# Image scale weights loaded and used in two column parts, with V rows between

## The chip, the cores and the metric

The kernel runs on one core of a Trainium2 chip. The time is device time in microseconds (us) of one execution, the median of several. A core has four compute engines that run their own instruction streams and meet at semaphores: TensorE (PE in the profile; its weight loads are PEld), VectorE (DVE), ScalarE (ACT) and GpSimd (POOL). SyncE (SP) issues most of the transfers (DMAs) between main memory and the on-chip buffer SBUF. TensorE writes into PSUM, in eight banks; VectorE and ScalarE copy from there.

## The reference

One attention block for an image stream and a text stream, batch B = 2, 256 image tokens and 32 text tokens per batch, D = 1152 channels, all bf16:

```python
mod_i = (silu(c) @ wmod_img)          # six D-wide parts; shift, scale, gate are used
hi = layernorm(x_img) * (1 + sci) + shi
qi, ki, vi = split(hi @ wqkv_img)     # the same for the text stream
p = softmax(concat(qt, qi) @ concat(kt, ki).T * D**-0.5)
a = p @ concat(vt, vi)
out_i = x_img + gai * (ai @ wo_img)   # the same for the text stream
```

The weights are read once each: fourteen blocks of 1152 x 1152, some 37 MB, through five SBUF slots of one block.

## The kernel before

D is cut into KT = 9 blocks of P = 128 channels. The image tokens of both batches are 512 columns, in four token tiles (`i` = 0 to 3; 0 and 1 are the first batch). A weight block is a tile of 128 partitions by 9 rows (`kt`) by 1152 columns; "row" below is one `kt`.

Transfers. All weight loads stand in one list on SP's queue (lines 97 to 115): the image tokens `x_i` in two pieces, the image scale weights `w_sc_i` in five row pieces (99 to 101), the V weights `w_v_i` in four (102, 103), then whole blocks: image shift `w_sh_i`, `w_q_i`, `w_k_i`, text shift, text scale, text q, k and v, the two gates, the two output blocks. A load into a slot waits until the slot's former user is done; a load also waits for the landing of an earlier load whose semaphore it takes over (eight loads before).

Order of the work. `pin` keeps an instruction at its place in its engine's program; matmuls (`mm`) and transposes (`tr`) are all pinned, so TensorE runs in the order of the source.

1. Warm-up matmuls on zeros (line 130, eight; line 145, fifteen) while `x_i` loads. `silu(c)` is computed and transposed into `sT`.
2. Layer norm of the image tokens (248 to 258). Tiles 0 and 2 get their sums on ScalarE (`ln_sums`, two activations), tiles 1 and 3 their statistics on VectorE (`ln_stats`, three `bn_stats` and an aggregate). `ln_norm` on VectorE writes the normalized tiles `xn_i`.
3. Transposes of `xn_i` by TensorE into PSUM, three channel blocks of one batch at a time (`x_transposes`), copied out into `xT_i`. Before, the three groups of the first batch go ahead of the scale matmuls and those of the second batch between them (259 to 272).
4. Image scale, `sc_cols`: 81 matmuls with two output columns each, 9 rows by 9 column blocks, accumulated in one PSUM bank `sc_ps`; `warm_up(3)` and `warm_up(1)` stand between the row pieces. Then VectorE adds 1 (273).
5. `x_scale` on VectorE multiplies the transposed tokens by 1 + scale into `hS_i`, one channel block of one batch at a time (274 to 280).
6. V: `v_open` multiplies `hS_i` with `w_v_i` into PSUM banks of 512 columns (281 to 284): A0 is token tiles 0 and 1 by two column chunks, A1 tiles 2 and 3 by the first chunk, six banks in all. The two left, (2,1) and (3,1), follow. `evac` copies a finished bank into `v_i`, alternately by VectorE and ScalarE.
7. Image shift (305, 306): `mod_rows_of(w_sh_i)` is 36 matmuls into `p_sh` (the group `gps` of the profile), transposed by VectorE into columns. They modulate `xT_i` in place on VectorE and ScalarE (310 to 317), and their product with `w_v_i` (`shift_v_rows`) makes up for the shift left out of V. The (2,1) bank runs around this stage (307, 319), (3,1) behind it.
8. q and k of the image, with the text stream's steps hooked in between, each with its own weight block: text shift, text scale, text q and k, v; then scores and softmax, the gate rows (`mod_rows`, again `gps`), attention and the output projections.

PSUM has two pools: `ps_mm` with six banks and `ps_tr` with two.

Of the kernel before, what the change touches and what calls it, by code (L numbers as in the profile page):

```python
# [8 lines left out]
ACT = mybir.ActivationFunctionType  # L9
ALU = mybir.AluOpType  # L10
# [4 lines left out]
def kernel(  # L15
# [14 lines left out]
    nc = tc.nc  # L30
    bf = mybir.dt.bfloat16
    f32 = mybir.dt.float32
    PSUM = bass.MemoryType.PSUM

    B, NI, D = x_img.shape
    NT = x_txt.shape[1]
    P = 128
    KT = D // P
# [4 lines left out]
    CH = 384  # L43
    NCH = D // CH
# [7 lines left out]
    const = ctx.enter_context(tc.tile_pool(name="const", bufs=1))  # L52
    work = ctx.enter_context(tc.tile_pool(name="work", bufs=2))
    small = ctx.enter_context(tc.tile_pool(name="small", bufs=4))
    ps_mm = ctx.enter_context(tc.tile_pool(name="ps_mm", bufs=6, space=PSUM))
    ps_tr = ctx.enter_context(tc.tile_pool(name="ps_tr", bufs=2, space=PSUM))

    pin = tc.keep_in_program_order

    def mm(*a, **k):  # L60
        return pin(nc.tensor.matmul(*a, **k))  # L61

    def tr(*a, **k):
        return pin(nc.tensor.transpose(*a, **k))  # L64
# [6 lines left out]
    x_i = act.tile([P, NIT, D], bf)  # L71
# [4 lines left out]
    def wtile(slot):  # L76
        return wpool.tile([P, KT, D], bf, tag="w%d" % slot, name="t")

    def wview(src, c0):
        return src.rearrange("(kt p) n -> p kt n", p=P)[:, :, c0:c0 + D]  # L80

    K8 = KT - 1

    def load_w(slot, src, c0, splits=(D,)):
        t = wtile(slot)
        sv = wview(src, c0)
        o = 0
        for n in splits:
            nc.sync.dma_start(t[:, :, o:o + n], sv[:, :, o:o + n])
            o += n  # L90
        return t

    w_sc_i = wtile(0)
    w_v_i = wtile(1)
    sc_v, v_v = wview(wmod_img, D), wview(wqkv_img, 2 * D)
    for b in range(B):
        nc.sync.dma_start(x_i[:, b * TPB:(b + 1) * TPB, :], x_img[b].rearrange("(p t) d -> p t d", t=TPB))  # L97

    SCC = (0, 3, 5, 7, K8, KT)
    for r0, r1 in zip(SCC, SCC[1:]):  # L100
        nc.sync.dma_start(w_sc_i[:, r0:r1, :], sc_v[:, r0:r1, :])  # L101
    for r0, r1 in ((0, 1), (1, 3), (3, 6), (6, KT)):
        nc.sync.dma_start(w_v_i[:, r0:r1, :], v_v[:, r0:r1, :])
    w_sh_i = load_w(2, wmod_img, 0)
    w_q_i = load_w(3, wqkv_img, 0)
    w_k_i = load_w(4, wqkv_img, D)
    w_sh_t = load_w(0, wmod_txt, 0)
    w_sc_t = load_w(1, wmod_txt, D)
# [17 lines left out]
    def warm_up(n):  # L126
        for _ in range(n):
            mm(wps[:], lhsT=warm[:, 0:P], rhs=warm[:], start=True, stop=True)
# [13 lines left out]
    sT_ps = ps_tr.tile([P, B * KT], bf, tag="tr")  # L142
    tr(sT_ps[:], s18[:], ident[0:B * KT, 0:B * KT])
    sT = const.tile([P, KT, B], bf)
    warm_up(15)

    def silu_cols():
        pin(nc.vector.tensor_copy(sT[:], sT_ps[:].rearrange("p (b kt) -> p kt b", b=B)))
# [4 lines left out]
    def evac(out_ap, in_ap):  # L153
        if evac_idx[0] % 2 == 0:
            nc.vector.tensor_copy(out_ap, in_ap)  # L155
        else:
            nc.scalar.copy(out_ap, in_ap)  # L157
        evac_idx[0] += 1

    def ln_stats(x_ap, np_, between=None):  # L160
        stats = small.tile([P, NCH, 6], f32, tag="stats")
        for k in range(NCH):
            if k == 1 and between:
                between()
            pin(nc.vector.bn_stats(stats[0:np_, k, :], x_ap[:, k * CH:(k + 1) * CH]))
        mv = small.tile([P, 2], f32, tag="mv")
        pin(nc.vector.bn_aggr(mv[0:np_, :], stats[0:np_, :, :]))
        return mv

    def ln_sums(x_ap, junk):  # L170
        sm = small.tile([P, 3], f32, tag="lnact")
        pin(nc.scalar.activation(junk, x_ap, ACT.Copy, scale=1.0 / D, accum_out=sm[:, 0:1]))
        pin(nc.scalar.activation(junk, x_ap, ACT.Square, scale=float(D) ** -0.5, accum_out=sm[:, 1:2]))
        return sm

    def ln_var(sm):
        pin(nc.vector.scalar_tensor_tensor(sm[:, 2:3], sm[:, 0:1], sm[:, 0:1], sm[:, 1:2],
                                           op0=ALU.mult, op1=ALU.subtract))
# [10 lines left out]
    xn_i = act.tile([P, NIT, D], bf, tag="A")  # L189
    hS_i = act.tile([P, KT, B * NI], bf, tag="Bt")  # L190
    xT_i = act.tile([P, KT, B * NI], bf)

    sc1_i = const.tile([P, KT, B], f32)
    qkT = act.tile([P, 2 * KT, B, NTOK], bf, tag="Q")

    sc_ps = ps_mm.tile([P, KT, B], f32, tag="mm")

    def sc_cols(r0, r1):
        for kt in range(r0, r1):
            for j in range(KT):  # L200
                mm(sc_ps[:, j, :], lhsT=w_sc_i[:, kt, j * P:(j + 1) * P], rhs=sT[:, kt, :],
                   start=(kt == 0 and j == 0), stop=(kt == KT - 1), skip_group_check=True)

    def x_transposes(k0, b):
        tr_pool = b == 0 and k0 < 6
        tp = (ps_tr if tr_pool else ps_mm).tile([P, 3, NI], bf, tag="tr" if tr_pool else "mm", name="tp")
        for kt in range(k0, k0 + 3):
            for t in range(TPB):
                i = b * TPB + t
                tr(tp[:, kt - k0, t * P:(t + 1) * P], xn_i[:, i, kt * P:(kt + 1) * P], ident[:])  # L210
        dst = xT_i[:, k0:k0 + 3, b * NI:(b + 1) * NI]

        def copy_out():
            pin(nc.scalar.copy(dst, tp[:]) if b == 0 or k0 == 6 else nc.vector.tensor_copy(dst, tp[:]))

        return copy_out

    def x_scale(k0, k1, b):
        for kt in range(k0, k1):
            pin(nc.vector.tensor_scalar(hS_i[:, kt, b * NI:(b + 1) * NI], xT_i[:, kt, b * NI:(b + 1) * NI],  # L220
                                        sc1_i[:, kt, b:b + 1], None, op0=ALU.mult))

    VW = 512
    v_i = act.tile([P, NIT, D], bf, tag="A")
# [2 lines left out]
    def v_open(ids, k0, k1, kt_major=True):  # L227
        for key in ids:
            if key not in accs:
                accs[key] = ps_mm.tile([P, VW], f32, tag="mm", name="vps")  # L230
        loop = [(kt, key) for kt in range(k0, k1) for key in ids] if kt_major else \
            [(kt, key) for key in ids for kt in range(k0, k1)]
        for kt, (i, cc) in loop:
            mm(accs[(i, cc)][:], lhsT=hS_i[:, kt, i * P:(i + 1) * P], rhs=w_v_i[:, kt, cc * VW:(cc + 1) * VW],
               start=(kt == 0), stop=(kt == KT - 1), skip_group_check=True)
            if kt == KT - 1:
                evac(v_i[:, i, cc * VW:(cc + 1) * VW], accs[(i, cc)][:])

    A0 = [(0, 0), (1, 0), (0, 1), (1, 1)]
    A1 = [(2, 0), (3, 0)]  # L240
# [4 lines left out]
    def ln_norm_act(i, sm):  # L245
        ln_norm(x_i[:, i, :], sm[:, 0:1], ln_rstd(sm[:, 2:3], P, sign=-1.0), P, xn_i[:, i, :])
# [3 lines left out]
    ln_var(s0)  # L250
    ln_norm_dve(1, m1)
    ln_norm_act(0, s0)
    s2 = ln_sums(x_i[:, 2, :], xn_i[:, 2, :])
    m3 = ln_stats(x_i[:, 3, :], P)
    ln_var(s2)
    r3, r2 = ln_rstd(m3[:, 1:2], P), ln_rstd(s2[:, 2:3], P, sign=-1.0)
    ln_norm(x_i[:, 3, :], m3[:, 0:1], r3, P, xn_i[:, 3, :])
    ln_norm(x_i[:, 2, :], s2[:, 0:1], r2, P, xn_i[:, 2, :])
    x_transposes(0, 0)()
    x_transposes(3, 0)()  # L260
    x_transposes(6, 0)()
    sc_cols(0, 3)
    warm_up(3)
    sc_cols(3, 5)
    warm_up(1)
    sc_cols(5, 7)
    x_transposes(0, 1)()
    out31 = x_transposes(3, 1)
    sc_cols(7, K8)
    sc_cols(K8, KT)  # L270
    out61 = x_transposes(6, 1)
    out61()
    pin(nc.vector.tensor_scalar_add(sc1_i[:], sc_ps[:], 1.0))
    x_scale(0, 3, 0)
    x_scale(0, 3, 1)
    out31()
    for b in range(B):
        x_scale(3, 6, b)
    for b in range(B):
        x_scale(6, KT, b)  # L280
    v_open(A0, 0, 3)
    v_open(A1, 0, 3)
    v_open(A0 + A1, 3, KT - 2)
    v_open(A0 + A1, KT - 2, KT, kt_major=False)

    NGG = 4
# [2 lines left out]
    def group(w, kt, g):  # L289
        return w[:, kt, :].rearrange("p (c g l) -> p g c l", g=NGG, l=LW)[:, g]  # L290

    def mod_rows_of(w, lhs):
        gps = ps_tr.tile([P, KT, LW], f32, tag="tr")
        for kt in range(KT):
            for g in range(NGG):
                mm(gps[LW * g:LW * g + LW], lhsT=lhs[:, kt, :], rhs=group(w, kt, g),
                   start=(kt == 0), stop=(kt == KT - 1), tile_position=(0, LW * g))
        return gps

    def mod_cols_of(gps, name):  # L300
        t = const.tile([P, KT, LW], f32, name=name)
        nc.vector.transpose(t[:].rearrange("p c l -> p (c l)"), gps[:].rearrange("p c l -> p (c l)"))
        return t

    p_sh = mod_rows_of(w_sh_i, sT32)
    sh_i = mod_cols_of(p_sh, "shc")
    v_open([(2, 1)], 0, 4)
    nc.vector.tensor_copy(shT32[:, :, 0:B], sh_i[:, :, 0:B])
    hT_i = xT_i
    for kt in range(KT):  # L310
        for b in range(B):
            h = hT_i[:, kt, b * NI:(b + 1) * NI]
            if b == 0 or kt % 3 == 0:
                nc.vector.tensor_scalar(h, h, sc1_i[:, kt, b:b + 1], sh_i[:, kt, b:b + 1],
                                        op0=ALU.mult, op1=ALU.add)
            else:
                nc.scalar.activation(h, h, ACT.Identity, bias=sh_i[:, kt, b:b + 1], scale=sc1_i[:, kt, b:b + 1])
    pin(nc.scalar.dma_start(x_t[:], xt_flat[:, :]))
    v_open([(2, 1)], 4, KT)
    v_open([(3, 1)], 0, KT)  # L320

    def v_last():
# [301 lines left out]
```

## Time and profile before

| | |
|---|---|
| median of five executions | 123.01 us (121.92 to 124.74) |
| the profiled execution | 121.92 us, span 120.1 us, mean granted TensorE clock 0.997 |
| TensorE busy | 113.7 us, 95% of the span |
| VectorE, ScalarE, GpSimd busy | 56.0, 34.5, 11.1 us |
| moved by DMA | 40.88 MB, mean 341 GB/s, about 410 GB/s until 98 us |
| first V matmul | 14.39 us |
| shift matmuls `gps` | 26.77 us |
| first q matmul | 35.20 us |

The span is the time from the first to the last instruction of the program; the execution takes 1.8 us more. A line of digits in the profile cuts the span in 40 slices and gives the busy share in tenths. Line 61 is the helper `mm`, so matmuls are told apart by the tiles they write. Ends of matmuls are modelled, starts are not; a row of n matmuls in the timeline runs to the end of its last one. In a row of a timeline, the engine, line, operation, output and inputs follow the start and the length, then the count. A row of DMA issues gives kilobytes and the time from issue to landing.

### The profile page before, as it was taken

Reading aid. Unit: us, or ns where it says so; the run is one execution under the profiler, and the core shown is the slowest. Engines: PE = TensorE matmul, PEld = TensorE weight load, DVE = VectorE, ACT = ScalarE, POOL = GpSimd, SP = SyncE. Lnnn points to the kernel's source line nnn. Section 1 sums busy time; section 2 is a strip of 40 time slices with the busy share of each in tenths; the row PEclk is TensorE's granted clock in tenths of the full one; section 3 lists DMA queues with packets and bytes.
Section 4 is the critical chain, followed back from the end, with each engine's and each line's share of the span. In section 5 each row is a group of like instructions: output and inputs, shape, how many; then the busy total and the mean of one; then the engine's idle time right before and its main releaser. Section 6 shows DMA issues by size and latency. Waiting matters only on the chain.

```text
span 120.1 us, 2599 instructions
## 1 busy us (share of the span) xinstructions
PE 113.7 (95%) x1112; PEld 67.4 (56%) x1121; DVE 56.0 (47%) x146; ACT 34.5 (29%) x73; POOL 11.1 (9%) x28
## 2 busy tenths in 40 slices
PE   5999899989999999999999999999999999999970
PEld 2248744435674444544548448486777766567650
DVE  1677590066837222131721203037885756666670
ACT  5799600054713103201011111125348610000000
POOL 7400000000000000000000000000222708000000
PEclk9999999999999999999999999999999999999998
DMA  3999999999999999999999999999999992420232
GB/s 129 372 389 389 406 405 408 416 408 415 403 369 412 404 409 414 411 411 412 407 411 411 418 401 414 411 405 411 411 400 411 411 359 68 138 98 0 98 81 72
DMA packets 18502, 40.88 MB, mean 341 GB/s; under 512 B 907, under 2 KB 1435, under 8 KB 18491
## 3 DMA queue, kind: packets, MB, share of 16 engines
q1 hardware_dynamic: 17616, 39.56, 84.6%
q0 software_dynamic: 480, 0.89, 2.2%
q10 hardware_dynamic: 395, 0.26, 0.7%
q8 instruction: 9, 0.15, 0.5%
q14 instruction: 2, 0.02, 0.0%
HBM read 39.38 MB, written 1.34 MB: 339 GB/s over the span
## 4 chain that ended last, share of the span: by engine, by line
PE 74%; DMA 20%; SPq 1%; DVE 1%; issue 1%
PE ps L61 51%; DMA t<-in_wmod_img_dram 20%; PE gps L61 6%; PE aps L61 6%; PE vps L61 5%; PE sps L61 4%; PE pT_ps L64 1%; SPq L97 1%; DVE tmp L565 1%; DVE o L566 0%; SPq L101 0%; PE tpt L64 0%
## 5 line engine op out<-in xcount | busy, mean ns | idle before, releaser
L61 PE MATMUL ps<-xT_i,t 128*128 128x512 bf16 x156 | 35.5, 379 | 0.4 <-issue 0.2
L61 PEld LDWEIGHTS <-t 128*128 128x128 bf16 x405 | 22.7, 98 | 19.3 <-issue 0.7
L61 PE MATMUL ps<-t,aT 128*128 128x384 bf16 (+3 forms) x153 | 20.2, 308 | 0.0
L61 PE MATMUL vps<-t,hS_i 128*128 128x512 bf16 (+1 forms) x106 | 17.8, 325 | 0.4 <-DVE hS_i L220 0.3
L61 PEld LDWEIGHTS <-aT 128*128 128x128 bf16 (+1 forms) x153 | 13.0, 101 | 7.1 <-issue 0.5
L61 PEld LDWEIGHTS <-hS_i 128*128 128x128 bf16 x108 | 9.0, 98 | 9.0 <-DVE hS_i L220 0.5
L155 DVE CAST qkT<-ps 128x512 bf16<-128x512 f32 (+1 forms) x6 | 3.8, 636 | 15.4 <-PE ps L61 15.4
L61 PE MATMUL wps<-warm 128*128 128x512 bf16 x26 | 8.9, 496 | 1.3 <-DVE warm L121 1.2
L435 POOL DMA_DIRECT2D mod_scratch<-g_sb x4 | 2.5, 633 | 80.1 <-ACT g_sb L157 80.1
L565 DVE TENSOR_TENSOR tmp<-ps,gb 128x384 bf16<-128x384 f32 (+2 forms) x13 | 6.8, 526 | 6.4 <-PE ps L61 6.3
L333 DVE TENSOR_SCALAR qkT<-ps 128x512 bf16<-128x512 f32 (+1 forms) x5 | 3.3, 665 | 10.8 <-PE ps L61 10.8
L335 ACT ACTIVATE qkT<-ps 128x512 bf16<-128x512 f32 (+1 forms) x6 | 3.3, 553 | 15.5 <-PE ps L61 15.5
L157 ACT CAST qkT<-ps 128x512 bf16<-128x512 f32 (+1 forms) x5 | 2.8, 565 | 16.6 <-PE ps L61 16.6
L155 DVE CAST v_i<-vps 128x512 bf16<-128x512 f32 x5 | 3.4, 689 | 7.9 <-PE vps L61 7.9
L61 PE MATMUL gps<-t,sT 128*32 128x288 bf16 x180 | 6.4, 287 | 0.5 <-DMA t<-in_wmod_img_dram 0.5
L61 PE MATMUL aps<-pT,v_i 128*128 128x288 bf16 x36 | 6.7, 287 | 0.0
L61 PEld LDWEIGHTS <-sT 128*32 128x32 bf16 x180 | 4.5, 96 | 2.5 <-issue 2.0
L61 PEld LDWEIGHTS <-warm 128*128 128x128 bf16 x27 | 2.9, 117 | 5.3 <-issue 2.9
L537 DVE TENSOR_SCALAR aT<-aps,svc 128x288 bf16<-128x288 f32 x9 | 4.7, 518 | 2.4 <-PE aps L61 2.3
L61 PE MATMUL sps<-qkT 128*128 128x288 bf16 (+1 forms) x54 | 5.5, 287 | 0.0
L157 ACT CAST v_i<-vps 128x512 bf16<-128x512 f32 x4 | 2.3, 586 | 10.6 <-PE vps L61 10.6
L539 ACT ACTIVATE aT<-aps,svc 128x288 bf16<-128x288 f32 x9 | 4.5, 502 | 2.5 <-PE aps L61 2.5
(94 smaller groups left out, 105.2 us busy)
## 6 DMA issues: line engine op xcount, KB each, us to landing
t<-in_wmod_txt_dram SPq DMA_DIRECT2D x3, 2592.0 KB, 18.9
t<-in_wqkv_txt_dram SPq DMA_DIRECT2D x3, 2592.0 KB, 15.5
t<-in_wmod_img_dram SPq DMA_DIRECT2D x2, 2592.0 KB, 18.9
t<-in_wqkv_img_dram SPq DMA_DIRECT2D x2, 2592.0 KB, 22.5
t<-in_wo_img_dram SPq DMA_DIRECT2D x1, 2592.0 KB, 18.2
t<-in_wo_txt_dram SPq DMA_DIRECT2D x1, 2592.0 KB
t<-in_wqkv_img_dram SPq DMA_DIRECT2D x2, 864.0 KB, 12.1
x_i<-in_x_img_dram SPq DMA_DIRECT2D x2, 576.0 KB, 4.1
```

The lines of the kernel that those rows point to most:

```text
L61: return pin(nc.tensor.matmul(*a, **k))
L64: return pin(nc.tensor.transpose(*a, **k))
L97: nc.sync.dma_start(x_i[:, b * TPB:(b + 1) * TPB, :], x_img[b].rearrange("(p t) d -> p t d", t=TPB))
L155: nc.vector.tensor_copy(out_ap, in_ap)
L157: nc.scalar.copy(out_ap, in_ap)
L333: nc.vector.tensor_scalar_mul(out_ap, in_ap, SCALE)
L335: nc.scalar.mul(out_ap, in_ap, SCALE)
L435: nc.gpsimd.dma_start(gsc[si, b, :].rearrange("(g j) -> g j", g=NGG), g_sb[b:P:32, :])
L537: nc.vector.tensor_scalar(dst, aps[:], bias, None, op0=ALU.add)
L539: nc.scalar.activation(dst, aps[:], ACT.Identity, bias=bias)
L565: nc.vector.tensor_mul(tmp[:, 0:n], ps[:, 0:n], gb[:, b, c0:c0 + n])
```

## The change

The image scale weights are split by columns: 640 (five column blocks, `KA`) and 512 (four). The loads become: part one in three row pieces, V rows 0 to 4 in three, part two in two, V rows 5 to 8 in two. `w_q_i` is loaded in two column pieces of 512 and 640. The scale matmuls of part one give 1 + scale for channel blocks 0 to 4, so that V rows 0 to 3 of the first batch run as soon as the first batch is scaled; the last statistics, the norms and the transposes of the second batch come behind them in the program. Part two of the scale follows four V rows of A1. The bank (2,1) runs whole before the shift matmuls. `sc_ps` moves to the pool `ps_tr`. Three warm-up matmuls are left out (15 become 13; 3 and 1 become 2 and 1), and the copies of transposed groups are shared out otherwise between VectorE and ScalarE.

```diff
-    SCC = (0, 3, 5, 7, K8, KT)
-    for r0, r1 in zip(SCC, SCC[1:]):
-        nc.sync.dma_start(w_sc_i[:, r0:r1, :], sc_v[:, r0:r1, :])
-    for r0, r1 in ((0, 1), (1, 3), (3, 6), (6, KT)):
-        nc.sync.dma_start(w_v_i[:, r0:r1, :], v_v[:, r0:r1, :])
+    KA = 5
+    CA = KA * P
+
+    def load_rows(t, sv, r0, r1, c0=0, c1=D):
+        nc.sync.dma_start(t[:, r0:r1, c0:c1], sv[:, r0:r1, c0:c1])
+
+    for r0, r1 in ((0, 4), (4, 7), (7, KT)):
+        load_rows(w_sc_i, sc_v, r0, r1, 0, CA)
+    for r0, r1 in ((0, 1), (1, 3), (3, KA)):
+        load_rows(w_v_i, v_v, r0, r1)
+    for r0, r1 in ((0, 5), (5, KT)):
+        load_rows(w_sc_i, sc_v, r0, r1, CA, D)
+    for r0, r1 in ((KA, 7), (7, KT)):
+        load_rows(w_v_i, v_v, r0, r1)
     w_sh_i = load_w(2, wmod_img, 0)
-    w_q_i = load_w(3, wqkv_img, 0)
+    w_q_i = load_w(3, wqkv_img, 0, (4 * P, 5 * P))
...
-    warm_up(15)
+    warm_up(13)
...
-    sc_ps = ps_mm.tile([P, KT, B], f32, tag="mm")
+    sc_ps = ps_tr.tile([P, KT, B], f32, tag="tr")
...
+    def sc_done(h):
+        pin(nc.vector.tensor_scalar_add(sc1[h][:], sc_ps[:, h * KA:h * KA + sc1[h].shape[1]], 1.0))
...
-            pin(nc.scalar.copy(dst, tp[:]) if b == 0 or k0 == 6 else nc.vector.tensor_copy(dst, tp[:]))
+            pin(nc.vector.tensor_copy(dst, tp[:]) if k0 == 3 else nc.scalar.copy(dst, tp[:]))
...
-    s2 = ln_sums(x_i[:, 2, :], xn_i[:, 2, :])
-    m3 = ln_stats(x_i[:, 3, :], P)
+    s2 = small.tile([P, 3], f32, tag="lnact")
+    act_sum(s2, x_i[:, 2, :], xn_i[:, 2, :], False)
+    st3 = small.tile([P, NCH, 6], f32, tag="stats")
+    bn_part(st3, x_i[:, 3, :], P, 0)
+    bn_part(st3, x_i[:, 3, :], P, 1)
+    out00, out30 = x_transposes(0, 0), x_transposes(3, 0)
+    out00()
+    out30()
+    out60 = x_transposes(6, 0)
+    act_sum(s2, x_i[:, 2, :], xn_i[:, 2, :], True)
+    sc_cols(0, 4, 0, KA)
+    warm_up(2)
+    sc_cols(4, 7, 0, KA)
+    warm_up(1)
+    sc_cols(7, KT, 0, KA)
+    sc_done(0)
+    x_scale(0, KA, 0)
+    out60()
+    bn_part(st3, x_i[:, 3, :], P, 2)
+    m3 = bn_done(st3, P)
     ln_var(s2)
     r3, r2 = ln_rstd(m3[:, 1:2], P), ln_rstd(s2[:, 2:3], P, sign=-1.0)
     ln_norm(x_i[:, 3, :], m3[:, 0:1], r3, P, xn_i[:, 3, :])
     ln_norm(x_i[:, 2, :], s2[:, 0:1], r2, P, xn_i[:, 2, :])
...
+    v_open(A0, 0, 4)
+    outs = [x_transposes(k0, 1) for k0 in (0, 3, 6)]
+    outs[0]()
+    outs[1]()
+    x_scale(0, KA, 1)
+    outs[2]()
+    v_open(A0, 4, KA)
+    v_open(A1, 0, KA - 1)
+    sc_cols(0, 5, KA, KT)
+    sc_cols(5, KT, KA, KT)
+    v_open(A1, KA - 1, KA)
+    sc_done(1)
+    for kt in range(KA, KT):
+        for b in range(B):
+            x_scale(kt, kt + 1, b)
+    v_open(A0 + A1, KA, KT - 2)
     v_open(A0 + A1, KT - 2, KT, kt_major=False)
...
+    v_open([(2, 1)], 0, KT)
     p_sh = mod_rows_of(w_sh_i, sT32)
     sh_i = mod_cols_of(p_sh, "shc")
-    v_open([(2, 1)], 0, 4)
...
-    v_open([(2, 1)], 4, KT)
     v_open([(3, 1)], 0, KT)
```

## The prediction

> **What bounds the kernel now.** I read the page first: which engine is full, and how full the transfers are.
>
> ```profile
> span 120.1 us, 2599 instructions
> PE 113.7 (95%) x1112; PEld 67.4 (56%) x1121; DVE 56.0 (47%) x146; ACT 34.5 (29%) x73; POOL 11.1 (9%) x28
> PE   5999899989999999999999999999999999999970
> DMA  3999999999999999999999999999999992420232
> ```
>
> Two resources run full side by side: TensorE to the end, and the 16 DMA engines until slice 33, about 98 us. The chain of waits, in order of time, says which leads where:
>
> ```profile
> 2.12 7.95 DMA t<-in_wmod_img_dram
> 10.08 16.64 DMA t<-in_wmod_img_dram
> 26.77 1.29 PE gps L61 x36
> ```
>
> Up to 26.77 us the chain is transfers, ending with the image shift weights `w_sh_i`; from there it is TensorE alone. So a gain has to come before 26.77 us, and it lasts only while each later weight matrix still lands before TensorE wants it. The timeline of the stretch that is rewritten (start, length, engine):
>
> ```profile
> 9.02 1.17 PE L64 MATMUL tp<-ident,xn_i 128*128 128x128 bf16 x18
> 10.02 0.82 PE L61 MATMUL sc_ps<-sT,t 128*128 128x2 bf16 x27
> 11.35 0.59 PE L61 MATMUL sc_ps<-sT,t 128*128 128x2 bf16 x18
> 11.80 0.38 PE L61 MATMUL wps<-warm 128*128 128x512 bf16 x1
> 12.02 0.59 PE L61 MATMUL sc_ps<-sT,t 128*128 128x2 bf16 x18
> 13.76 0.18 DVE L273 TENSOR_SCALAR sc_i<-sc_ps 128x18 f32<-128x18 f32 x1 [0.21 <-PE sc_ps L61]
> 14.05 1.27 DVE L220 TENSOR_SCALAR hS_i<-xT_i,sc_i 128x256 bf16<-128x256 bf16 x6
> 14.39 11.83 PE L61 MATMUL vps<-t,hS_i 128*128 128x512 bf16 x53 [0.31 <-DVE hS_i L220]
> 26.77 1.29 PE L61 MATMUL gps<-t,sT 128*32 128x288 bf16 x36 [0.55 <-DMA t<-in_wmod_img_dram]
> ```
>
> Starts give the true pace, as ends are modelled: 18 transposes from 9.02 to 10.02, 0.0556 us each; 18 scale matmuls from 11.35 to 11.80, 0.025 each; a warm-up matmul 0.216 (11.80 to 12.02), and a 512-column V matmul the same (53 starts in 11.83 less the last one's 0.38). TensorE is not waiting for the scale weights here: from 9.02 to 13.9 it runs without a gap, and four warm-up matmuls in it (0.86 us) are filler. Idle are 0.5 us before V (sum, +1, first scaled tile) and 0.55 us before `gps`.
>
> **The change, TensorE's work step by step.** Nothing useful is added: 36 transposes, 81 scale matmuls and all V work stay. Removed are two warm-ups ahead of the first transpose and one between.
> - Start. The second of the two normalized tiles ends at 8.43 on VectorE; the first transpose starts at 9.02, behind the warm-ups. Two fewer (0.43) bring it to 8.59, still 0.16 behind the tile; the first V weight load needed 0.06 after its scaled tile (14.05 + 0.28 to 14.39). Gain 0.43.
> - 18 transposes to 9.59; 20 scale matmuls 10.09; 2 warm-ups 10.52; 15 more 10.90; 1 warm-up 11.11; the last 10 end at 11.36.
> - The +1 and the scaling: before, the last scale matmul started at 13.56 and V at 14.39, 0.83 later. Now 11.34 + 0.83 = 12.17. V starts 2.2 us earlier.
> - V rows 0 to 3 for four accumulators: 16 x 0.216 = 3.45, to 15.62. Moved under it: VectorE scales 5 tiles (1.27/6 each) to 12.9, then the last statistics 0.5, aggregate and norms; in the trace the second norm ends 1.92 after the statistics (9.86 to 11.78), so 15.3, plus 0.06. The second batch's transposes can start at 15.4, wanted at 15.62: cover with 0.2 to spare; each further 0.1 on VectorE costs 0.1.
> - 18 transposes to 16.62, row 4 to 17.48. The first copy-out takes 0.80 on ScalarE from 16.16, so the first second-batch tile is scaled by 17.4: just in time. The last copy-out ends at 17.7 and may give the second A1 accumulator its bank: 0.05.
> - 8 V matmuls 19.25, 36 scale matmuls 20.15, 2 V matmuls 20.58. The second +1 again needs 0.83 after the last scale matmul: 20.96, so 0.38 idle remains after that cover.
> - 24 matmuls to 26.14. Then the whole (2,1) accumulator, 9 x 0.216, to 28.08, before `gps`, which waits for nothing if `w_sh_i` is there by then. `gps` takes 1.22, to 29.30. Before, the same work was done at 26.77 + 1.22 + 1.94 = 29.93. **Gain 0.63 us**, nearly all of it the wait for `w_sh_i`.
>
> Behind `gps`: the shift columns and the modulation now start 1.3 later and end near 33.2 instead of 31.93 (33.9 with a V eviction in between); q needs them at 34.6. What hides them is (3,1), the last V columns and the V shift rows, 5.3 us; without it they cost 3.9. The text rows' load on ScalarE's queue goes out 1.3 later too, and lands near 36.5 instead of 35.2; its statistics on VectorE started at 36.16 and are needed at 46.97. Nothing.
>
> **The change, the transfers.** Bytes are the same; part one lands sooner, all later loads somewhat later, since rows of 2304 bytes become two packets (1280 and 1024), in the scale weights and in `w_q_i`. No load of the trace has such packets. The nearest rows are the page's queue totals, and below them the last stores by themselves (116.9 to 117.6 us):
>
> ```profile
> q1 hardware_dynamic: 17616, 39.56, 84.6%
> q10 hardware_dynamic: 395, 0.26, 0.7%
> q1 hardware_dynamic: 130, 0.17, 69.0%
> ```
>
> Packet times: 84.6% of 16 x 120.1 us over 17616 is 92 ns for 2246 bytes; q10 34 ns for 658; the stores 59 ns for 1308 (69% of 16 x 0.7 us over 130). A line through the first two has 10 ns that doesn't shrink with size, through the first and third 13.5. An engine moves 72 rows of a matrix: 0.7 to 1.0 us for each split matrix. The Trainium skill (DMA: Bandwidth & Descriptors, "Why small descriptors are slow (HBM only)") gives 3 cycles a packet beside one for each 32 bytes: 72 + 3 before, 40 + 3 and 32 + 3 after, 4% of 92 ns, 0.26 us a matrix. I take 0.7, the row; by the rule the later loads are 0.5 us late in all, by mine 1.4, by the upper line 1.9. Below nothing it can't be: the engines are full and the bytes equal.
>
> The same page's rules for authors want 1 MiB or more in a DMA, which speaks against the smaller pieces (288 to 720 KB). By its sum (2.0 us each, end to end) they would be slow one by one; but the trace's 288 KB pieces (issued at 3.20 and 3.71, 9.0 and 9.2 to landing) land 0.7 apart, the rate of the larger ones. Pieces in a full queue cost nothing; only packets do.
>
> Landings: scale part one at 864 KB by 8.64 was 24 packets an engine; 32, 24 and 16 packets of 57 ns from the same start give 8.2, 9.5, 10.4, ahead of 9.59, 10.52, 11.11. V rows 0, 1-2, 3-4 at 11.1, 12.5, 14.0, wanted at 12.17, 13.0, 14.8. Part two near 16.7 and 18.2 (wanted 19.25), the other V rows by 21 (22 and on). `w_sh_i` 26.73 + 0.7 = 27.4, wanted 28.08. `w_q_i`'s first 512 columns near 31, the rest 35.1, wanted 34.6 and 42.3. SP's queue keeps its order, and its waits for old landings (eight loads back) end well ahead of the data.
>
> Then the loads behind. The window of each issue gives its landing; the tightest is the text gate `w_ga_t`, issued at 66.14:
>
> ```profile
> t<-in_wmod_txt_dram SPq DMA_DIRECT2D x1, 2592.0 KB, 19.7
> 87.75 1.29 PE L61 MATMUL gps<-t,sT 128*32 128x288 bf16 x36
> ```
>
> It lands at 85.85 and is wanted at 87.75: 1.9 us spare. The text shift weights have 2.5 (46.9, halfway between neighbours' 40.4 and 53.3, and 49.38), the others 3.2 or more. After: landing 87.25, wanted 87.12. That wait gives 0.13 back. **Net 0.5 us.**
>
> **The sum.** The profiled execution took 121.92 for a span of 120.1; 121.92 - 0.5 = 121.4. It was also the fastest of the five, whose median is 123.01; the difference carried over gives 122.5.
>
> **Rivals.**
> - Faster by over 1%: the profile shows the fastest execution. If in the median one the extra 1.1 us is weights landing late, `w_sh_i` holds TensorE longer there, and the 0.7 us of room ahead of the new `gps` takes that off as well: 0.5 + 0.7, about 121.8, to 121.2. For it: the chain to 26.77 is transfers alone. Against: late weights also eat `w_ga_t`'s room.
> - No gain: VectorE's chain (0.2 to spare) or the first copy-out is late by 0.5: 123.0. For it: both margins are thinner than one VectorE instruction. Then `w_sh_i` no longer matters, as `gps` comes at 28.6.
> - Slower: the packets. Every ns beyond the bytes' share costs 0.144 us on all loads behind `w_q_i`, and TensorE stands at the text gate (the place is the 87.75 line). It decides from 1.9 us of delay, 13 ns a packet, for any loss; the upper line (13.5 ns) is there already. If a half row took two thirds of a whole one, 31 ns more, the loads are 4.5 late, less 1.9 is 2.6: 125.6; at 23 ns 1.4: 124.4. For it: DMA engines are full to 98 us, so nothing is caught up. Against: the stores' packets cost only 59 ns.
>
> **How the numbers follow.** A time 1% off is about what a measurement of this kernel can tell from no change. Likeliest, gain 0.2 to 1.0: 0.38, 122.0 to 122.8. Faster rival 0.20. No gain, from 0.2 faster to 1.2 slower: 0.14. Slower rival 0.28. Likeliest 122.5; faster by over 1% 0.20, within 0.52, slower 0.28. Range 121.3 to 124.9: it leaves out 0.04 of the faster rival and 0.15 of the slower one.
>
> **What would show it.** First transpose near 8.6; first V matmul at 12.2; second batch's transposes near 15.6 with no idle before them; idle of 0.4 ahead of V row 5; `gps` at 28.1 with no wait for `w_sh_i`; q near 34.6; packets of 1280 and 1024 bytes at 57 and 47 ns; `w_ga_t` landing at 87.2. Wrong if V waits for rows, if the granted clock falls between 9 and 12 us, or if TensorE stands before the text shift rows or the gate.

## The result, and the profile after

After the change the kernel takes 121.67 us (median of 43 executions, 121.25 to 122.62); the kernel before, over the 80 executions beside them, 122.13 (121.48 to 124.74). The ratio is 0.9962, 95% interval 0.9948 to 0.9976: faster by 0.46 us, under half a per cent. The forecast was 122.5 with a gain of 0.5. The gain is right to a tenth; the absolute number is 0.8 high because it was hung on the median of five executions (123.01), and 80 of them have a median 0.9 lower. Of the 182 executions of the kernel before that stand beside the experiments, 27 had a mean granted clock under 0.992 (median 123.61 us), of the changed kernel's 66 one, of the 32 of the move alone (e1 and e10 below) seven; the ratios leave out the slow ones, the medians do not.

The profiled execution of after took 121.91 us, the one of before 121.92. The two profiles differ by nothing in total, and yet by much inside: the one of before lies 0.2 us under its kernel's median, the one of after 0.2 over. From the page of after, whose span is 120.0 us:

```profile
PE 113.1 (94%) x1108; PEld 66.8 (56%) x1118; DVE 56.4 (47%) x147; ACT 34.4 (29%) x73; POOL 11.1 (9%) x28
...
q1 hardware_dynamic: 19952, 39.56, 85.8%
```

TensorE does 0.6 us less (the three warm-ups) in the same span. The load queue carries the same 39.56 MB in 2336 packets more, 146 for each of the 16 DMA engines. The timeline of TensorE in after (start, length, group, idle time before it):

```profile
8.42 1.18 PE L64 MATMUL tp<-ident,xn_i 128*128 128x128 bf16 x18
...
12.01 1.04 PE L61 MATMUL vps<-t,hS_i 128*128 128x512 bf16 x4 [0.66 <-DVE hS_i L247]
13.34 2.75 PE L61 MATMUL vps<-t,hS_i 128*128 128x512 bf16 x12 [0.29 <-DMA t<-in_wqkv_img_dram]
15.92 1.17 PE L64 MATMUL tp<-ident,xn_i 128*128 128x128 bf16 x18
...
28.37 1.29 PE L61 MATMUL gps<-t,sT 128*32 128x288 bf16 x36
...
87.41 1.29 PE L61 MATMUL gps<-t,sT 128*32 128x288 bf16 x36
89.05 0.42 PE L61 MATMUL aps<-pT,v_i 128*128 128x288 bf16 x2 [0.36 <-DVE pT L558]
```

V starts 2.4 us sooner than before (12.01 against 14.39), has to wait for V rows 1 and 2 (0.29 us idle by the profile, 0.47 by the starts, since four matmuls take 0.86 of the 1.33 from 12.01 to 13.34), and the shift rows' `gps` at 28.37 waits for nothing; before it waited 0.55. The text gate's `gps` stands at 87.41 against 87.75, so 0.34 us of lead got there. Attention starts at 89.05, where it started before: the lead is gone within 1.6 us. The chain of waits of after (start, length, what led) shows what has taken the place of the scale and shift weights:

```profile
3.77 9.53 DMA t<-in_wqkv_img_dram
13.34 2.75 PE vps L61 x12
...
20.80 0.30 DVE hS_i L247
21.14 0.39 PE vps L61
...
28.44 1.22 PE gps L61 x36
...
85.15 0.60 ACT e L512 x2
...
88.48 0.52 DVE pT L558
```

The chain is transfers only up to 13.34 us (V rows 1 and 2), no longer up to 26.77. TensorE has one gap left in the rewritten stretch, ahead of V row 5 (20.60 to 21.14: the second +1 and one scaled tile). And a second thing is new: from 81.18 to 89.01 us the chain now runs through the softmax on ScalarE and VectorE (the last two lines are of it). In before it stayed on TensorE there.

### The profile page after: what moved, and what is told of

It reads as the page before. It is cut to its first block, busy times and chain, and to the rows that moved or that the text cites. A ratio compares the mean times of both kernels' runs of the same rounds, so it can differ in the third digit from the quotient of the medians.

```text
span 120.0 us, 2594 instructions
## 1 busy us (share of the span) xinstructions
PE 113.1 (94%) x1108; PEld 66.8 (56%) x1118; DVE 56.4 (47%) x147; ACT 34.4 (29%) x73; POOL 11.1 (9%) x28
## 3 DMA queue, kind: packets, MB, share of 16 engines
q1 hardware_dynamic: 19952, 39.56, 85.8%
## 4 chain that ended last, share of the span: by engine, by line
PE 78%; DMA 8%; DVE 6%; SPq 2%; ACT 2%; issue 1%; ACTq 0%
PE ps L61 51%; PE vps L61 14%; DMA t<-in_wqkv_img_dram 8%; PE aps L61 6%; PE gps L61 4%; SPq L103 2%; ACT e L512 2%; DVE nmx L509 1%; DVE pb L516 1%; PE tp L64 1%; PE sc_ps L61 1%; DVE pb L518 1%; SPq L97 1%; PE sps L61 1%; DVE rs L514 1%
## 5 line engine op out<-in xcount | busy, mean ns | idle before, releaser
L61 PE MATMUL wps<-warm 128*128 128x512 bf16 x23 | 8.0, 500 | 1.3 <-DVE warm L130 1.2
L61 PE MATMUL aps<-pT,v_t 128*128 128x288 bf16 x18 | 5.1, 286 | 0.0
```

## Experiments

Two theories of the gain. **The move**: TensorE has nothing to do while `w_sh_i` arrives; putting the (2,1) accumulator ahead of `gps` fills that wait, and the split of the scale weights is only what fills the time before. **The early V**: starting V 2.2 us sooner is what pays. And two of what could eat it: the packets of the half rows, and the filler that was taken out.

### The move alone, the split alone

The kernel before with the (2,1) accumulator whole ahead of the shift rows, nothing else (e1; e10 is the same kernel again):

```diff
+    v_open([(2, 1)], 0, KT)
     p_sh = mod_rows_of(w_sh_i, sT32)
     sh_i = mod_cols_of(p_sh, "shc")
-    v_open([(2, 1)], 0, 4)
...
-    v_open([(2, 1)], 4, KT)
```

> The kernel before, with one edit: the accumulator (2,1) runs whole ahead of the image shift rows. My theory (the gain is the wait for the shift weights, and any TensorE work put ahead of it collects it): V ends at 26.0 as before, (2,1) at 28.0, the shift rows start at 28.0 with no wait and end at 29.3 instead of 29.9; ratio to before about 0.995, the whole gain of the change without any column split. Rival (the split and the early V rows make the gain): the move alone gives nothing, ratio 1.000.

> The kernel before with the move of (2,1) alone, again. If the column split is worth nothing beside the move: 0.995 to 0.998, no different from the changed kernel. If the split adds to it: 0.998 or more, with the changed kernel lower by 0.2% or more.

Measured: 0.9958 [0.9933, 0.9983] and 0.9943 [0.9900, 0.9986]. The medians of all their executions, 121.99 and 122.00 us, are 0.3 above the change's. The timeline of e1:

```profile
28.45 1.29 PE L61 MATMUL gps<-t,sT 128*32 128x288 bf16 x36
34.95 5.35 PE L61 MATMUL ps<-xT_i,t 128*128 128x512 bf16 x23
```

With the V start where it was (14.47), `gps` waits for nothing, and q starts at 34.95 against 35.20. The 0.25 us of lead last: attention starts at 88.79 against 89.05. By the ratios the move alone gives as much time as the whole change: they can't be told from 0.9962. The profile of e10 shows none of this gain; there V waits for its rows, `gps` comes at 29.19 and q only at 35.68:

```profile
16.36 12.89 PE L61 MATMUL vps<-t,hS_i 128*128 128x512 bf16 x59 [0.92 <-DMA t<-in_wqkv_img_dram]
```

The counterpart is the changed kernel with (2,1) back in its two old places (e3):

```diff
-    v_open([(2, 1)], 0, KT)
     p_sh = mod_rows_of(w_sh_i, sT32)
     sh_i = mod_cols_of(p_sh, "shc")
+    v_open([(2, 1)], 0, 4)
...
+    v_open([(2, 1)], 4, KT)
```

> The changed kernel with (2,1) back in its old place: four rows behind the shift rows, the rest behind the modulation. Split, early V rows and fewer warm-ups stay. My theory: V ends near 26.4, the shift weights land at 27.1 (0.4 later than before, by the packets), so the shift rows wait about 0.7 us and start 0.4 later than in the kernel before; ratio to before about 1.003. Rival (early V is the gain): ratio 0.996, as with the whole change.

Measured: 1.0095 [1.0059, 1.0130], 123.17 us. One line of its timeline says why:

```profile
27.77 1.29 PE L61 MATMUL gps<-t,sT 128*32 128x288 bf16 x36 [1.77 <-DMA t<-in_wmod_img_dram]
```

V is early here too, and all that it wins stands as a wait of 1.77 us at `w_sh_i`. These weights land at 27.73, against 26.73 in before. The extra packets are part of that second: with the same loads they land at 27.15 in after, so the packets leave some 0.6 us of it unexplained. Expected was 1.003; 0.34 us of the loss is the late exponential told below, which e3 has too. An early V is worth nothing by itself; it is worth what work can be put ahead of the next weight matrix.

### The warm-ups

Two experiments on the filler. e2 is the kernel before with two fewer ahead of the transposes and one fewer between the scale rows, as in the change (the first diff); e4 has the move of e1, and no filler between the scale rows at all (the second, without the move's lines):

```diff
-    warm_up(15)
+    warm_up(13)
...
-    warm_up(3)
+    warm_up(2)
```

```diff
-    warm_up(15)
+    warm_up(13)
...
-    warm_up(3)
...
-    warm_up(1)
```

> The kernel before with 13 and 2 warm-up matmuls in place of 15 and 3, nothing else. My theory: TensorE is 0.4 to 0.6 us earlier up to the end of V (25.5), and then waits that much longer for the shift weights, which still land at 26.7; ratio 1.000. Rival (TensorE's order before V sets the time): first transpose at 8.6 and everything after it earlier by 0.4 to 0.6 us, ratio 0.996.

> The kernel before with (2,1) ahead of the shift rows, 13 warm-up matmuls in place of 15, and the four between the scale matmuls left out; no column split. My theory: with the shift weights out of the way TensorE's own filler counts; the last scale row lands at 12.9, so V starts near 14.0 instead of 14.4, the shift rows near 27.6; ratio to before 0.991 to 0.993, and the tightest later load (text gate, 1.9 us spare) is not reached. Rival (the clock needs the filler): the granted clock drops near 11 us, V starts at half pace, ratio 1.00 or more.

Measured: e2 1.0006 [0.9975, 1.0037]; e4 1.0036 [1.0010, 1.0061], 122.89 us, so about 0.8% above the same move with its filler. The timeline of e2:

```profile
11.97 0.60 PE L61 MATMUL sc_ps<-sT,t 128*128 128x2 bf16 x18 [0.40 <-DMA t<-in_wmod_img_dram]
...
26.72 1.29 PE L61 MATMUL gps<-t,sT 128*32 128x288 bf16 x36 [0.22 <-DMA t<-in_wmod_img_dram]
```

The 0.4 us that e2 gains at the transposes is a wait for scale rows at 11.97, and V starts at 14.40, as before. So the filler in the kernel before covered a wait for the scale weights that its trace could not show. In e10, where the transposes happened to start at 8.25, the same wait (0.39 us at 11.81) shows with all the filler in place. In after TensorE does not wait for scale rows: part one is five ninths of the bytes. In e4, whose timeline and windows follow, both covers are gone:

```profile
10.36 0.60 PE L61 MATMUL sc_ps<-sT,t 128*128 128x2 bf16 x18 [0.32 <-DMA t<-in_wmod_img_dram]
11.84 0.60 PE L61 MATMUL sc_ps<-sT,t 128*128 128x2 bf16 x18 [0.87 <-DMA t<-in_wmod_img_dram]
```

```profile
12.60:16.00 3.40, 3.40 (x38) 2.31 (x36) 2.45 (x10) 1.09 (x2) 0.00 (x0) 0.50 1.04 407
16.00:20.00 4.00, 3.95 (x19) 1.80 (x19) 2.37 (x13) 0.00 (x0) 0.00 (x0) 1.00 1.04 407
```

The column behind the five engines is the granted TensorE clock: 0.50 from 12.6 to 16.0 us, 1.00 in the window behind it. V starts at 14.62 and runs its first 1.4 us at half pace, which is 0.7 us lost. All 22 executions of e4 have a mean clock under 0.992. That is the rival of e4's expectation, and not its theory. Whether the filler that the change keeps could go was not run.

### The order of part two, and the size of part one

The idle 0.4 us ahead of V row 5 comes from part two's sum being late. e5 (again as e11) puts part two after two rows of A1 rather than four; e6 makes part one four column blocks wide, with its matmuls arranged to suit:

```diff
     v_open(A0, 4, KA)
-    v_open(A1, 0, KA - 1)
+    v_open(A1, 0, 2)
     sc_cols(0, 5, KA, KT)
     sc_cols(5, KT, KA, KT)
-    v_open(A1, KA - 1, KA)
+    v_open(A1, 2, KA)
```

```diff
-    KA = 5
+    KA = 4
...
-    v_open(A0, 4, KA)
-    v_open(A1, 0, KA - 1)
     sc_cols(0, 5, KA, KT)
+    v_open(A1, 0, 2)
     sc_cols(5, KT, KA, KT)
-    v_open(A1, KA - 1, KA)
+    v_open(A1, 2, KA)
```

> The changed kernel with part two of the scale matmuls after the first two A1 rows instead of the first four, so three rows of A1 (6 matmuls, 1.3 us) lie between it and V row 5 instead of one (0.43). My theory: the idle ahead of row 5 (about 0.5 us in the changed kernel's profile) is gone, the shift rows start near 27.9 instead of 28.4, still behind the landing of their weights at 27.2; ratio to the kernel before 0.992 to 0.993. Rival (a later wait takes it back: the text gate's weights or the softmax chain on VectorE): same ratio as the changed kernel, 0.996.

> The changed kernel with part two of the scale matmuls two A1 rows earlier, again. If the idle ahead of V row 5 counts: ratio 0.992 to 0.994, below the changed kernel by 0.2% or more. If not: the same as the changed kernel.

> The changed kernel with part one of four column blocks instead of five (512 and 640 columns), V rows 0 to 3 behind it, and part two's matmuls in two pieces: one ahead of A1, one behind its first two rows. My theory: 288 KB less ahead of the V rows bring them 0.7 us earlier, so the 0.5 us wait for V rows 1 and 2 is gone too; V starts near 11.8, the shift rows near 27.5; ratio 0.989 to 0.992 unless the text gate's weights (about 86.8, wanted then near 86.5) stop it. Rival (the transposes of the second batch come late, since VectorE sets their time): 0.996.

Measured: e5 0.9960 [0.9932, 0.9987], e11 0.9960 [0.9941, 0.9980], e6 0.9982 [0.9964, 1.0000]. In the trace e5 and e11 do what they should: q starts at 34.40 and 34.23, against 34.87 in after, and the medians of their spans are 119.5 us, against 119.75. But the ratios are those of the change, so both expectations (0.994 or less) missed, and that gain is not shown by time. e6 starts V only 0.12 sooner (11.89). Its q comes as early as in e5 (34.50), yet its ratio is on the wrong side of after; why was not followed up.

### The packets

e7 is the changed kernel with `w_q_i` loaded in whole rows again (the first diff); e8 goes the other way and loads four more matrices behind it in two halves of 576 columns each, which adds 288 packets to each DMA engine (the second):

```diff
-    w_q_i = load_w(3, wqkv_img, 0, (4 * P, 5 * P))
+    w_q_i = load_w(3, wqkv_img, 0)
```

```diff
-    w_k_i = load_w(4, wqkv_img, D)
-    w_sh_t = load_w(0, wmod_txt, 0)
-    w_sc_t = load_w(1, wmod_txt, D)
-    w_q_t = load_w(2, wqkv_txt, 0)
+    w_k_i = load_w(4, wqkv_img, D, (576, 576))
+    w_sh_t = load_w(0, wmod_txt, 0, (576, 576))
+    w_sc_t = load_w(1, wmod_txt, D, (576, 576))
+    w_q_t = load_w(2, wqkv_txt, 0, (576, 576))
```

> The changed kernel with the image q weights loaded whole instead of in columns of 512 and 640. My theory: they land near 33.8, still ahead of 34.9, and all later loads come 0.4 to 0.7 us sooner, which nothing waits for; ratio 0.996, as the changed kernel. Rival (the split is needed): q waits for its weights, ratio 0.998 or more; rival (the packets already cost time later): 0.993.

> The changed kernel with four more weight blocks loaded in two column halves of 576 (image k, text shift, text scale, text q): 288 more packets an engine, the slower rival of the prediction enlarged. My theory (10 ns a packet): all loads behind are 2.9 us late; the text scale and text q weights just make it, the text gate's (86.8 in the changed kernel, wanted at 87.4) land at 89.7 and hold TensorE about 2.2 us; ratio about 1.014. By the 3 cycles a packet (3.6 ns) they are 1.0 late, 87.8, and the ratio is 0.999 to 1.000. Rival (packets are free when the queue is full): 0.996.

Measured: e7 0.9974 [0.9953, 0.9995], e8 1.0010 [0.9988, 1.0031]. In e8's expectation, the 3 cycles a packet are those of the page that the prediction names, the Trainium skill's DMA: Bandwidth & Descriptors. One line of e7's timeline and one of e8's:

```profile
34.80 1.90 PE L61 MATMUL ps<-xT_i,t 128*128 128x512 bf16 x8 [0.31 <-DMA t<-in_wqkv_img_dram]
```

```profile
88.72 1.29 PE L61 MATMUL gps<-t,sT 128*32 128x288 bf16 x36 [1.38 <-DMA t<-in_wmod_txt_dram]
```

In e7 q comes at 33.21 + 1.22 = 34.4 and waits 0.3 to 0.4 us for its weights: the split of `w_q_i` is needed once q starts that early, though its worth is too small for the ratios. In e8 the text gate stands 1.38 us. That is the mechanism of the rival that ended slower, at its place. It needed 432 extra packets for each engine to get there, where the change has 144. The gate weights are issued at 65.74 us in e7 and at 66.36 in e8; their issues, e7's first:

```profile
t<-in_wmod_txt_dram SPq DMA_DIRECT2D x1, 2592.0 KB, 21.1
t<-in_wmod_txt_dram SPq DMA_DIRECT2D x1, 2592.0 KB, 22.3
```

So they land at 86.84 and 88.66: 1.8 us for 360 more packets, 5 ns a packet. That is one pair of profiles, and landings differ among kernels with the same loads by some tenths (the gate weights land at 85.84 in before and at 86.33 in e1). Other pairs give other figures. `w_sh_i`, with 72 extra packets ahead of it, lands at 27.15 in after and 27.33 in e9, against 26.73 in before and 26.91 in e1: 0.4 us, 6 ns a packet. The 72 packets that e7 saves bring the image gate's weights no sooner (80.33, against 80.39 in after and 80.16 in e9). So 5 ns is good to a few ns.

### The changed kernel again

e9 is the changed kernel without an edit, beside e10 and e11 on one chip.

> The changed kernel again, beside the next two on one chip. Expected: ratio to before 0.996; in its profile the shift rows near 28.3, q near 34.8, and the softmax chain 0.3 to 0.4 us earlier than in the kernel before; if that chain stands at the same time as before again (attention at 89.05 in both first profiles), the gain is lost there as a rule and not by chance.

Measured: 0.9968 [0.9949, 0.9987]. In its profile V has no wait for rows 1 and 2, q starts at 34.74, the gate stands at 87.28 and attention starts at 88.93: 0.47 ahead of before at the gate, 0.12 at the attention. So the wait for V rows comes and goes, and the loss between gate and attention does not. The packets do not make that wait, as e9 has the same: in after the first scale piece lands at 8.66 and V rows 1 and 2 at 13.29, in e9 at 7.90 and 12.62, and V starts at 12.33 there.

### The loss ahead of the attention

From the gate's `gps` to the first attention matmul it is 1.30 us in before (87.75 to 89.05) and 1.64 in after. Three pairs of lines from the timelines show where: the maximum of the second image tile's scores (VectorE) and the exponential that waits for it (ScalarE), the softmax's third after the text's and the first image tile's. Before, with the first attention matmul:

```profile
84.61 0.44 DVE L474 TENSOR_REDUCE nmx<-sps 128x1 f32<-128x288 f32 x1
85.14 0.50 ACT L477 ACTIVATE e<-sps,nmx 128x288 f32<-128x288 f32 x1 [0.99 <-DVE nmx L474]
...
89.05 0.42 PE L61 MATMUL aps<-pT,v_i 128*128 128x288 bf16 x2
```

After:

```profile
84.27 0.44 DVE L509 TENSOR_REDUCE nmx<-sps 128x1 f32<-128x288 f32 x1
85.15 0.50 ACT L512 ACTIVATE e<-sps,nmx 128x288 f32<-128x288 f32 x1 [1.33 <-DVE pb L518]
```

Before, the exponential starts 0.09 us after the maximum ends (84.61 + 0.44); in after 0.44 us. The profile names a later VectorE instruction (`pb`), but only as the one that ended last; the exponential does not read it. The trace's records of ScalarE say more. A separate instruction waits for the maximum, and it is through at 84.76 in after and at 85.10 in before, each time about 0.05 us after the maximum. The exponential behind it then starts 0.05 us later in before and 0.39 us later in after. Its own wait is for an earlier result of ScalarE, of 83.81 at the latest. So nothing that it waits for is late.

The gap is 0.42 to 0.44 in the profile of every kernel with the split up to here (after, e3, e5 to e9, e11) and 0.09 to 0.10 in every one without (before, e1, e2, e4, e10), so neither chance nor the clock makes it. What differs on ScalarE is one instruction: with the split its first shift activation (L353) has two semaphores to wait for, and a separate wait instruction stands ahead of it. In the trace's records of ScalarE, counted from the first, the exponential is the 64th instead of the 63rd (the 59th and 58th of the next expectation leave out five, at the start and for issues of transfers). e12 is e5 with one copy-out of a K block given to VectorE, 15 us earlier, where both engines idle. That makes it the 63rd again:

```diff
+    EV_DVE = 27
     def evac(out_ap, in_ap):
-        if evac_idx[0] % 2 == 0:
+        if evac_idx[0] % 2 == 0 or evac_idx[0] == EV_DVE:
             nc.vector.tensor_copy(out_ap, in_ap)
```

> The version of e5 with one instruction fewer on ScalarE: the copy-out of one K block (it ran on ScalarE near 69 us, where both engines idle for over 3 us between blocks) is done by VectorE. With it the third image softmax exp stands at the same place in ScalarE's program as in the kernel before (the 58th instruction, not the 59th). Theory A: the 0.34 us by which that exp starts late in every kernel with the split belongs to its place in ScalarE's instruction stream (instructions arriving in blocks, the exp being the first of one). Then the exp starts 0.09 us after its max ends, as before, the attention starts 0.34 us earlier, the span is about 119.1 us and the ratio about 0.993. Theory B: it belongs to something else that the split does (buffers, transfers, the order of events). Then the exp starts 0.43 us after its max as in e5, span 119.5 us, ratio 0.996. Theory C: the stall goes, but another wait takes the time (the copy of the probabilities by VectorE, or the next exp): exp 0.09 us after its max and a span of 119.4 to 119.6 us all the same.

Measured: 0.9902 [0.9864, 0.9940], 121.23 us (120.89 to 121.59). Its timeline:

```profile
83.88 0.44 DVE L510 TENSOR_REDUCE nmx<-sps 128x1 f32<-128x288 f32 x1
84.42 0.50 ACT L513 ACTIVATE e<-sps,nmx 128x288 f32<-128x288 f32 x1 [0.99 <-DVE nmx L510]
...
87.02 1.29 PE L61 MATMUL gps<-t,sT 128*32 128x288 bf16 x36
88.32 0.42 PE L61 MATMUL aps<-pT,v_i 128*128 128x288 bf16 x2
```

The exponential starts 0.10 us after its maximum, gate to attention is 1.30 us, and no wait stands ahead of the attention. Of the three theories B fails, as the stall goes with an edit that leaves the split in place, and so does C, as all of it comes back. The lead at the gate is 0.73 us against before (87.02, 87.75), at the attention also 0.73. The median is 0.33 us under that of e5 (121.56) and 0.26 under that of e11 (121.49), about the size of the stall; the ratio looks better than that because the kernel before beside e12 took 122.28. This is the fastest kernel of the study, 0.4 us under the change (121.67).

What is shown is that the stall goes when one instruction is taken from ScalarE 15 us ahead. That it is the count that matters, as theory A has it, rests on this one edit, which also puts one instruction more ahead of VectorE's maximum. Why that place costs 0.34 us stays open. No transfer of instructions stands beside it: the trace of after has none between 79 and 87 us.

## Why the prediction was right, point by point

- **The filler.** "TensorE is not waiting for the scale weights here" was a wrong reading of a trace without gaps: e2 shows a wait of 0.40 us under the warm-ups. It cost the sum nothing, since part one of the split lands before its matmuls.
- **Start and V.** First transposes at 8.59 forecast, 8.42 seen; V at 12.17 forecast, 12.01 seen. The difference between last scale matmul and V, taken over from before as 0.83, held. The start itself varies: 8.75 and 12.33 in e9.
- **V rows.** "12.5, wanted at 13.0" for rows 1 and 2 was mis-sized in that profile: they landed at 13.29, a wait of 0.47 by the starts, and 0.29 of it stays in `gps`. This is one of the things that the prediction named as a sign of being wrong. It came true there without upsetting the time; e9's profile, where the rows land at 12.62, has no such wait.
- **The second batch under V rows 0 to 3.** 15.62 forecast, 15.92 seen: 12.01, the 16 matmuls' 3.45 and the 0.47 of the V wait. The cover of 0.2 us held: TensorE does not wait for the second batch's tiles.
- **Idle ahead of row 5.** 0.38 forecast; the chain has 0.54 from the +1 to the first matmul of row 5, of which the last row 4 matmuls cover part. Between 20.42 and `gps` at 28.37 TensorE has 35 matmuls of 0.216, so 0.39 of idle time. In e5 nearly all of it is gone.
- **`gps` and the gain.** 28.08 forecast, 28.37 seen, 28.24 in e9; no wait, as forecast. Its end, with (2,1) done by then, was 29.93 before and is 28.37 + 1.22 = 29.59: 0.34 us gained for 0.63 forecast, the rest, 0.29, being the V wait (0.47 less the earlier start). That the gain hangs on the wait for `w_sh_i` is shown from both sides: the move alone gives 0.9958 and 0.9943, the split without it 1.0095.
- **The gate.** "0.13 back" did not happen: the gate's `gps` follows the transposes at 87.41 with no idle. The packet times themselves came out as forecast: in after's trace packets of 1280 and 1024 bytes take 57 and 46 ns on average (57 and 47 forecast), 10 ns more together than a whole row's 94. What was mis-sized is the step from there to the landings, which come some 5 ns later for each extra packet. In a full queue packet times add up to more than the time there is (104.7% of the 16 engines between 9 and 27 us of after, 103.2% in before), so packets overlap, and their sum is not the delay of later loads. The Trainium skill's 3 cycles a descriptor (DMA: Bandwidth & Descriptors, "Why small descriptors are slow (HBM only)"), 3.6 ns here by the prediction's estimate, lie nearer to the landings than the 10 ns, but these are not exact enough to confirm them.
- **What no step had.** 0.34 us at the third softmax exponential, a change on an engine that the sum left out because it had slack everywhere. In after's own profile it cancels the lead at the gate: 0.34 gained by then, no gate wait, 0.34 lost again. So the steps as measured do not add up to the 0.5; that the net came out right on the medians is in part luck.
- **The rivals.** The faster one (weights late in the median execution) lost its ground: the median of 80 executions is only 0.2 above the profiled one, not 1.1. The slower one was real in kind, as e8 shows, and decides at three times the packets. What "no gain" named, thin margins on VectorE and the copy-out, held in after's profile and in e9's.

By its medians the change gains 0.46 us, by the single pair of profiles 0.01, by e9's profile 0.12 at the attention. Executions of one kernel differ by more than these differences, so the 0.46 is not split into its parts better than to some tenths.

## What to carry to other kernels

When the chain of waits says that a transfer leads, look for work that can be put ahead of the instruction that waits, before restructuring what comes sooner: here the move of nine matmuls bought, by the ratios, what the whole rewrite bought, and the rewrite without the move lost. What the rewrite adds shows only in e12, without the stall and with part two earlier: attention at 88.32, against 88.79 in e1, though the intervals of their ratios still overlap. Filler between small matmuls may be hiding a wait that the trace can't show; take it out in one run before costing an edit that relies on its being free. After an edit, compare the same instruction's distance to its releaser in both traces even on engines with slack: here one became 0.34 us late on the critical path, and an edit 15 us ahead on the same engine made it punctual again.

## What the runs showed of the hardware that was not expected

- The granted clock fell to 0.50 for 3.4 us in e4, after two waits of 0.32 and 0.87 us among two-column matmuls. The Trainium skill (TensorE: Matmul & The Clock Gate, "What's actually happening") lets it fall after an idle window of about 3.4 us; no idle time near that length is in the trace. TensorE was busy for 2.22 of the 3.41 us ahead of the fall; in e2, with 2.94 us busy between the same times, the clock stayed at 1.00. So a thinly filled window can be enough here; where the limit lies was not measured. The length of the fall agrees with the page's window.
- ScalarE's exponential started 0.42 to 0.44 us after its maximum, not 0.09 to 0.10, in all eight profiles where it is ScalarE's 64th record, and in none of the six where it is the 63rd. The cause is open.
- A row cut in two delayed later loads by about 5 ns for each extra packet (e7 to e8), half of the 10 ns that the packets' own times grow by.
